# Denominator loads on SP's queue, and a ring model that shares by packet size, in a gated attention and GLU kernel

## Chip, cores and metric

The kernel runs on one core of one Trainium2 chip, as one program. The metric is the device time in microseconds, the median of several runs.

## What is computed

Two branches read the same input x (2048 tokens, 640 features) and are mixed by a gate per token. Branch a is linear attention with 32 heads of 20 columns; branch b is a GLU with a sigmoid gate, 1536 wide.

```python
def _A_ref(x, wqkv, wo):
    B, S, D = x.shape
    H = 32; Dh = D // H
    qkv = (x @ wqkv).reshape(B, S, 3, H, Dh).transpose(2, 0, 3, 1, 4)
    q, k, v = qkv[0], qkv[1], qkv[2]
    phi = lambda t: jnp.where(t > 0, t + 1, jnp.exp(t)) + 1e-6
    pq, pk = phi(q), phi(k)
    kv = jnp.einsum("bhsd,bhse->bhde", pk, v)
    z = jnp.einsum("bhsd->bhd", pk)
    num = jnp.einsum("bhqd,bhde->bhqe", pq, kv)
    den = jnp.einsum("bhqd,bhd->bhq", pq, z)[..., None] + 1e-6
    o = num / den
    return o.transpose(0, 2, 1, 3).reshape(B, S, D) @ wo

def _B_ref(x, w_gate, w_up, w_down):
    g = jnp.einsum("bsd,df->bsf", x, w_gate)
    u = jnp.einsum("bsd,df->bsf", x, w_up)
    h = _sigmoid(g) * u
    return jnp.einsum("bsf,fd->bsd", h, w_down)

g = _sigmoid((x * gate_w).sum(-1, keepdims=True))
return g * a + (1 - g) * b
```

## The kernel before

**Tiling and stages.** The 2048 tokens are four groups g of 512 (NG, TG), the 640 features five tiles of 128 (KC). Each large product is split into a high and a low part (`split`) and runs as three matmuls (`mm3`, lines 404 to 406); products of 2x2 blocks are made with seven products instead of eight, out of sums of tiles. In order of time:

- the first part: keys, phi(k) and the matrix `gt`; the sum of phi(k) gathers in `zacc`;
- `q_phase(1)` and `f_phase(1)`: queries and GLU for groups 2 and 3. The transformed weights are written to DRAM (`w_dram`, `wd_dram`);
- `q_phase(0)` and `f_phase(0)`: the same for groups 0 and 1. The weights come back from DRAM ready made, by `load_form` (tiles wg, wu, ws for step f) and `load_wf` (tile wf, the down weights of two steps);
- the attention output: phi(q), scaled by gate / denominator, times the matrix `m`.

An f_phase runs over f = 0 to 11, each a block of seven steps s1 to s7. For odd f above 1 the four pieces d0 to d3 of the down product of the previous two steps lie between them; they use wf. At f, steps 2, 6 and 7 the loads of wg, wu and ws for f + 2 are issued, and after step 7 of an odd f `load_wf`.

**The denominators.** `phi_q` writes phi(q) of tile u and group g to `p_dram`. `queue_dens(g, g')` (line 1399) puts the work for two groups in a row: `load` fetches a tile of phi(q) as `pden` (256 KB), `one` multiplies it by the column `zcol` and adds it to `fac[:, g]` on DVE and then asks for the tile after the next, five times; after the fifth the result goes to `den_dram`. `turn_in` reads it back with four small loads (64 KB each, pieces of 512 bytes) that put heads on other partitions, and loads `gs`, the gate. `factor` adds, inverts, multiplies by the gate and stores `fac_dram`; `turn_out` reads that back with four small loads on SP. It is called in `f_phase(0)` at f = 3 for groups 2 and 3 and at f = 7 for groups 0 and 1 (`dens`, line 2011). `queue_scale` uses the factors much later.

**What sets the order.** TensorE's order stands in the program text. The work of ACT and DVE waits in lists and is put between the matmuls by `Order`, while the program is written and not on the chip: it keeps a clock for each engine (`pe`, `act`, `vec`), and `fill` (line 115) takes the next piece if its operands are there by the plan (`ready`) and if it ends by the plan less than a slack after TensorE's clock (`_fits`). The denominators are in the list `chain`, the last but one; behind it in `spare` are the pieces of `queue_m`, which load `mr` tiles on SP. Within an engine the order on the chip is then fixed: an engine that waits for an operand holds up all that is written behind it.

**DMA queues in the plan.** There are two, SP's (`sp`) and POOL's (`gp`), each a `Ring` that issues its transfers in the order of the text. A transfer that must wait for a tile or for data holds up those behind it. `Ring.dma_start` works out when it is issued and how long it takes alone (`took`, from its bytes and the length r of its contiguous pieces); `Rings.issue` then runs both rings against each other and sets the time of landing that `order.when` returns. While both have a transfer under way, each has half of the engines.

```python
dt = min([left[k] * len(live) for k in live] + [c - t for c in coming])
...
took = 1.25 * max(1, n // r) * (7 + 0.0377 * r) / 16e3
```

Of the kernel before, what the change touches and what calls it, by code (L numbers as in the profile page):

```python
# [14 lines left out]
P = 128  # L15
# [287 lines left out]
class Rings:  # L303
# [1 line left out]
    def __init__(self):  # L305
        self.q = [[], []]

    def issue(self, n, arrive, took):
        cell = [0.0]
        self.q[n].append((arrive, took, cell))  # L310
        i, t, left = [0, 0], 0.0, [None, None]
        q = self.q
        while True:
            for k in range(2):
                if left[k] is None and i[k] < len(q[k]) and q[k][i[k]][0] <= t:
                    left[k] = q[k][i[k]][1]
            live = [k for k in range(2) if left[k] is not None]
            coming = [q[k][i[k]][0] for k in range(2) if left[k] is None and i[k] < len(q[k])]
            if not live:
                if not coming:  # L320
                    break
                t = min(coming)
                continue
            dt = min([left[k] * len(live) for k in live] + [c - t for c in coming])
            t += dt
            for k in live:
                left[k] -= dt / len(live)
                if left[k] <= 1e-9:
                    q[k][i[k]][2][0] = t + 0.5
                    left[k] = None  # L330
                    i[k] += 1
        return cell


class Ring:

    def __init__(self, engine, order, rings, n, issue, lag):
        self.engine, self.order, self.rings, self.n, self.issue, self.lag = engine, order, rings, n, issue, lag
        self.t = 0.0
# [12 lines left out]
    def dma_start(self, out, src, **kw):  # L352
        o = self.order
        start = max(self.t, o.data(out, [src]))
        self.t = start + self.issue
        (r1, n), (r2, _) = (self.run(ap, 0 if getattr(ap.tensor, "_space", DRAM) == DRAM else 1) for ap in (out, src))
        r = min(r1, r2)
        took = 1.25 * max(1, n // r) * (7 + 0.0377 * r) / 16e3
        self.cell = self.rings.issue(self.n, start + self.lag, took)
        o.put(out, [src], self.cell)  # L360
        return self.engine.dma_start(out, src, **kw)

# [5 lines left out]
def v_cost(w):  # L368
    return 0.07 + w / 960

@with_exitstack
def gated_mix_kernel(ctx: ExitStack, tc: tile.TileContext, xt, xn, wk, wv, wo, wst_q, wst_f, out_t):
# [8 lines left out]
    sp, gp = Ring(nc.sync, order, rings, 0, 0.38, 1.5), Ring(nc.gpsimd, order, rings, 1, 0.55, 2.2)  # L381
# [37 lines left out]
    def vec2(out, a, b, op, after=""):  # L419
        order.on_vec(width(out), after, 1.0, out, a, b)  # L420
        nc.vector.tensor_tensor(out, a, b, op=op)  # L421

    def vec3(out, a, scalar, b, op0, op1, after=""):
        order.on_vec(width(out), after, 1.0, out, a, b)
        nc.vector.scalar_tensor_tensor(out, a, scalar, b, op0=op0, op1=op1)

    def vec1(out, a, s0, s1=None, op0=OP.mult, op1=None, after=""):
        order.on_vec(width(out), after, 1.0, out, a)
        if op1 is None:
            nc.vector.tensor_scalar(out, a, s0, None, op0=op0)  # L430
        else:
            nc.vector.tensor_scalar(out, a, s0, s1, op0=op0, op1=op1)
# [10 lines left out]
    def add(out, a, b, after=""):  # L443
        vec2(out, a, b, OP.add, after)

    def sub(out, a, b, after=""):
        vec2(out, a, b, OP.subtract, after)
# [7 lines left out]
    fac = common.tile([P, NG, TG], F32, name="fac")  # L455
    p_dram = dram.tile([P, KC, NG, TG], F32, name="p_dram")
# [76 lines left out]
    class Chunk:  # L533
# [39 lines left out]
        def sum(self, n):  # L573
            x = self.x
            b11, b12, b21, b22 = x[0][:, 0:2], x[1][:, 0:2], x[0][:, 2:4], x[1][:, 2:4]
            self.T = (b11, b22, b12, b21)
            if n == 0:
                sub(b11, b12, b11)
            elif n == 1:
                sub(b12, b22, b12)  # L580
            elif n == 2:
                sub(b22, b22, b11)
            else:
                sub(b21, b21, b22)
# [434 lines left out]
    g = GTBatch(0, [0])  # L1019
# [8 lines left out]
    for c in range(1, 4):  # L1028
        ck = chunks[c]
        if c == 1:  # L1030
# [14 lines left out]
            g = GTBatch(c, batches[c])  # L1045
# [97 lines left out]
        if c > 1:  # L1143
            g = GTBatch(c, batches[c])
# [50 lines left out]
    def tt(name, dt=F32, shape=(P, TG)):  # L1195
        return pw.tile(list(shape), dt, name=name, tag="t", bufs=4)
# [202 lines left out]
    def queue_dens(*gs2):  # L1399

        st = {}

        def load(g, u):
            if u < KC:
                st[g, u] = tt("pden")
                gp.dma_start(st[g, u], p_dram[:, u, g])
                st["at", g, u] = lambda: order.when(st[g, u])

        def one(g, u):
            td = fac[:, g]  # L1410
            if u == 0:
                vec1(td, st[g, u], zcol[:, 0:1], zeps[:, 0:1], OP.mult, OP.add)
            else:
                vec3(td, st[g, u], zcol[:, u:u + 1], td, OP.mult, OP.add)
            load(g, u + 2)
            if u == KC - 1:
                gp.dma_start(den_dram[:, g], td)
                st["at", g, u + 1] = lambda: order.when(den_dram[:, g])

        def turn_in(g):  # L1420
            for j in range(4):
                js = slice(j * H, (j + 1) * H)
                gp.dma_start(fac[js, g].rearrange("h (d c) -> h d c", c=P),
                                  den_dram[:, g, j * P:(j + 1) * P].rearrange("(d h) c -> h d c", h=H))
            st[g, "gs"] = tt("gs")[:, :P]
            sp.dma_start(st[g, "gs"], gate_rep[4 * g:4 * g + 4].rearrange("i h c -> (i h) c"))
            st["at", g, KC + 1] = lambda: max(order.when(fac[:, g]), order.when(st[g, "gs"]))

        def factor(g):
            td = fac[:, g]  # L1430
            q = td[:, :P]
            add(td[:, :2 * P], td[:, :2 * P], td[:, 2 * P:])
            add(q, q, td[:, P:2 * P])
            order.on_vec(5 * P, "")
            nc.vector.reciprocal(q, q)
            vec2(q, q, st[g, "gs"], OP.mult)
            gp.dma_start(fac_dram[:, g], q)
            st["at", g, KC + 2] = lambda: order.when(fac_dram[:, g])

        def turn_out(g):  # L1440
            for d in range(4):
                sp.dma_start(fac[d * H:(d + 1) * H, g].rearrange("h (j c) -> h j c", c=P),
                                  fac_dram[:, g].rearrange("(j h) c -> h j c", h=H))
        order.add(0, 0, lambda: [load(g, u) for u in range(2) for g in gs2], chain=True)
        for u in range(KC):
            for g in gs2:
                order.add(0, v_cost(TG), lambda g=g, u=u: one(g, u), None, lambda g=g, u=u: st["at", g, u](), chain=True)
        for n, (v, fn) in enumerate(((0, turn_in), (2.0, factor), (0, turn_out))):
            for g in gs2:
                order.add(0, v, lambda g=g, fn=fn: fn(g), ("fac", g) if n == 2 else None,  # L1450
                          lambda g=g, n=n: st["at", g, KC + n](), chain=True)
# [751 lines left out]
    q = q_phase(1, lambda k: [(b12h[:, k], b12l[:, k])], extra)  # L2203
# [33 lines left out]
    q = q_phase(0, lambda k: [(c_h[c][:, k], c_l[c][:, k]) for c in range(2)], {})  # L2237
# [383 lines left out]
```

## Time and profile before

| what | us |
|---|---|
| median of 3 runs (lowest to highest) | 735.46 (735.04 to 735.61) |
| the profiled execution | 735.37 |
| its span | 733.6 |
| TensorE (PE) busy | 727.4 |
| VectorE (DVE) busy | 561.5 |
| ScalarE (ACT) busy | 358.6 |
| GpSimd (POOL) busy | 114.0 |

Times within the trace count from the start of the span. `f_phase(0)` with the denominators lies at about 420 to 625 us in it. In a row of the order of time, the first figure is the start, the second the duration, and what stands in square brackets is how long the engine was idle before it and what ended that. In a row of the waits, the figures are the total, the number of times and the longest. A row that begins with SPq or POOL and DMA_DIRECT2D is the issue of a transfer; the landing comes later. The rows of DMA issues end with the median time to landing. In a row of windows follow, after the stretch and its length, the busy times (with the number of instructions) of PE, the weight loads, DVE, ACT and POOL, then TensorE's granted clock, the busy share of the DMA engines and GB/s.

### The profile page before, as it was taken

The numbers are of one execution on the slowest core, as the hardware profiler recorded it, in microseconds if no ns is written. First come the engines' busy times: TensorE is split into PE (matmuls) and PEld (weight loads), VectorE is DVE, ScalarE is ACT, GpSimd is POOL, SyncE is SP. The second block draws the span as 40 slices with busy tenths as digits, with TensorE's granted clock in tenths as the row PEclk, the third lists the DMA queues.
The fourth block names the chain that finished last, engine by engine and source line by source line (L and its number), as shares of the span: only waits on it lengthen the run. The fifth ranks groups of instructions, "written<-read, shape, count | busy, mean of one in ns | idle before, by whom it ended". The sixth has DMA issues, their size and how long they took to land.

```text
span 733.6 us, 10128 instructions
## 1 busy us (share of the span) xinstructions
PE 727.4 (99%) x3575; PEld 623.3 (85%) x3575; DVE 561.5 (77%) x987; ACT 358.6 (49%) x668; POOL 114.0 (16%) x197
## 2 busy tenths in 40 slices
PE   9999999999999999999999999999999999999998
PEld 8999999988788888888888888888787888888886
DVE  4978787987677989898989973466766775688783
ACT  5765648358556653535355363454333232324550
POOL 0211111113211211111210033023011331000000
PEclk9999999999999999999999999999999999999999
DMA  8464648697877866457687289878968597759212
GB/s 270 119 189 120 186 108 250 151 334 284 295 271 264 327 240 242 183 215 257 256 326 265 102 291 373 321 240 280 363 242 326 172 324 204 273 207 347 76 69 101
DMA packets 68873, 173.54 MB, mean 237 GB/s; under 512 B 11690, under 2 KB 31418, under 8 KB 65238
## 3 DMA queue, kind: packets, MB, share of 16 engines
q1 hardware_dynamic: 50342, 103.70, 42.7%
q0 software_dynamic: 18336, 69.03, 26.7%
q8 instruction: 28, 0.46, 0.3%
q14 instruction: 23, 0.19, 0.1%
q10 hardware_dynamic: 144, 0.16, 0.1%
HBM read 103.96 MB, written 63.92 MB: 229 GB/s over the span
## 4 chain that ended last, share of the span: by engine, by line
PE 86%; DMA 6%; issue 4%; DVE 2%; ACT 1%; POOL 1%; SPq 0%; POOLq 0%; ACTq 0%; DVEq 0%
PE ch L404 9%; PE ch L406 9%; PE ch L405 9%; PE cc L404 7%; PE cc L405 7%; PE cc L406 7%; PE dd L404 7%; PE dd L406 7%; PE dd L405 7%; PE rot L404 6%; PE rot L406 5%; PE rot L405 5%; DMA mr<-m_dram 2%; DMA pden<-p_dram 2%; DMA wg<-wf 1%
## 5 line engine op out<-in xcount | busy, mean ns | idle before, releaser
L417 ACT ACTIVATE c<-ch 128x512 f32<-128x512 f32 x52 | 31.1, 598 | 91.4 <-PE ch L406 91.3
L421 DVE TENSOR_TENSOR hf<-c,hf 128x512 fp32r<-128x512 f32 x75 | 51.2, 688 | 21.1 <-ACT hf L417 20.7
L417 ACT ACTIVATE hf<-c 128x512 fp32r<-128x512 f32 x75 | 46.1, 624 | 26.0 <-DVE c L421 26.0
L421 DVE TENSOR_TENSOR c<-cc,c 128x512 f32<-128x512 f32 x40 | 27.6, 689 | 40.6 <-PE cc L406 29.2
L404 PE MATMUL ch<-xth,ws 128*128 128x512 f32 x112 | 43.8, 391 | 0.0
L406 PE MATMUL ch<-xth,ws 128*128 128x512 f32 x112 | 43.6, 389 | 0.0
L405 PE MATMUL ch<-xtl,ws 128*128 128x512 f32 x112 | 43.6, 389 | 0.0
L421 DVE TENSOR_TENSOR tb<-rot,tb 128x512 f32<-128x512 f32 (+1 forms) x61 | 39.5, 677 | 3.0 <-PE rot L406 3.0
L421 DVE TENSOR_TENSOR tb<-dd,tb 128x512 f32<-128x512 f32 x44 | 30.3, 688 | 9.4 <-PE dd L406 9.4
L404 PE MATMUL dd<-xrh,wg 128*128 128x512 f32 x90 | 35.2, 391 | 0.0
L406 PE MATMUL dd<-xrh,wg 128*128 128x512 f32 x90 | 35.1, 389 | 0.0
L405 PE MATMUL dd<-xrl,wg 128*128 128x512 f32 x90 | 35.0, 389 | 0.0
L417 ACT ACTIVATE c<-dd 128x512 f32<-128x512 f32 x22 | 13.1, 598 | 41.4 <-PE dd L406 41.4
L404 PE MATMUL cc<-xbh,ws 128*128 128x512 f32 x84 | 32.7, 389 | 0.0
L405 PE MATMUL cc<-xbl,ws 128*128 128x512 f32 x84 | 32.7, 389 | 0.0
L406 PE MATMUL cc<-xbh,ws 128*128 128x512 f32 x84 | 32.7, 389 | 0.0
L421 DVE TENSOR_TENSOR c<-c,c 128x512 f32<-128x512 f32 x46 | 31.6, 688 | 1.3 <-ACT c L417 0.7
L417 ACT ACTIVATE dd<-ch 128x512 f32<-128x512 f32 x22 | 12.8, 582 | 35.0 <-PE ch L406 35.0
L421 DVE TENSOR_TENSOR wst<-wst 128x256 f32<-128x256 f32 (+2 forms) x69 | 27.4, 413 | 1.5
L404 PE MATMUL rot<-pkh,xnh 128*128 128x320 f32 x90 | 28.1, 312 | 0.1
L405 PE MATMUL rot<-pkl,xnh 128*128 128x320 f32 x90 | 27.8, 309 | 0.0
L406 PE MATMUL rot<-pkh,xnl 128*128 128x320 f32 x90 | 27.8, 309 | 0.0
(650 smaller groups left out, 2350.8 us busy)
## 6 DMA issues: line engine op xcount, KB each, us to landing
wf<-ws POOLq DMA_DIRECT2D x12, 1152.0 KB, 7.7
ws<-wf SPq DMA_DIRECT2D x11, 1152.0 KB, 9.5
wst<-wst_f SPq DMA_DIRECT2D x12, 640.0 KB, 5.2
wf<-wg POOLq DMA_DIRECT2D x12, 640.0 KB, 6.4
wd<-wd POOLq DMA_DIRECT2D x12, 640.0 KB, 8.0
wg<-wf SPq DMA_DIRECT2D x12, 640.0 KB, 5.8
wf<-wd SPq DMA_DIRECT2D x10, 640.0 KB, 10.1
xnst<-xn SPq DMA_DIRECT2D x16, 320.0 KB, 4.3
```

What stands on the lines that cost most here:

```text
L404: nc.tensor.matmul(out, l_hi, r_hi, start=first, stop=False, skip_group_check=True)
L405: nc.tensor.matmul(out, l_hi, r_lo, start=False, stop=False, skip_group_check=True)
L406: nc.tensor.matmul(out, l_lo, r_hi, start=False, stop=last, skip_group_check=True)
L417: nc.scalar.activation(out, src, fn, **kw)
L421: nc.vector.tensor_tensor(out, a, b, op=op)
```

## The change

Three things change. The model of the rings shares the engines between two live transfers in proportion to a weight, 7 + 0.0377 r with r taken as at most 2600 bytes, in place of equal halves. The `pden` loads, twenty in all, are issued on SP's queue in place of POOL's. So are the sixteen loads of `turn_in`. The stores to `p_dram`, `den_dram` and `fac_dram` stay on POOL's queue.

```diff
-    def issue(self, n, arrive, took):
+    def issue(self, n, arrive, took, share):
         cell = [0.0]
-        self.q[n].append((arrive, took, cell))
+        self.q[n].append((arrive, took, cell, share))
...
-            dt = min([left[k] * len(live) for k in live] + [c - t for c in coming])
+            all_ = sum(q[k][i[k]][3] for k in live)
+            part = {k: q[k][i[k]][3] / all_ for k in live}
+            dt = min([left[k] / part[k] for k in live] + [c - t for c in coming])
             t += dt
             for k in live:
-                left[k] -= dt / len(live)
+                left[k] -= dt * part[k]
...
-        self.cell = self.rings.issue(self.n, start + self.lag, took)
+        self.cell = self.rings.issue(self.n, start + self.lag, took, 7 + 0.0377 * min(r, 2600))
...
         def load(g, u):
             if u < KC:
                 st[g, u] = tt("pden")
-                gp.dma_start(st[g, u], p_dram[:, u, g])
+                sp.dma_start(st[g, u], p_dram[:, u, g])
...
             for j in range(4):
                 js = slice(j * H, (j + 1) * H)
-                gp.dma_start(fac[js, g].rearrange("h (d c) -> h d c", c=P),
+                sp.dma_start(fac[js, g].rearrange("h (d c) -> h d c", c=P),
                                   den_dram[:, g, j * P:(j + 1) * P].rearrange("(d h) c -> h d c", h=H))
```

## Prediction

> **What bounds the kernel now.** The page first, for the engine that is full; then what that engine waited for; then the stretch around each wait on the engine that released it, and last the two DMA queues there.
>
> ```profile
> span 733.6 us, 10128 instructions
> PE 727.4 (99%) x3575; PEld 623.3 (85%) x3575; DVE 561.5 (77%) x987; ACT 358.6 (49%) x668; POOL 114.0 (16%) x197
> PE rot L404 <- DVE tb L421: 0.9, 1, 0.9
> PE rot L492 <- PEq L2612: 0.8, 1, 0.8
> PE ch L404 <- ACT cx L417: 0.4, 1, 0.4
> PE dd L404 <- DMA wf<-wd: 0.2, 1, 0.2
> PE dd L404 <- ACT ms L417: 0.2, 1, 0.2
> ```
>
> TensorE is the bound: 727.4 of 733.6 us. The change adds and removes no matmul, so it can only fill or open gaps between matmuls. The waits are few: 0.8 us is the start, and 1.7 us lie inside, in four places. These figures are too small, because a matmul lasts 0.39 us in this trace while the next one starts 0.23 us after it, so 0.16 us of every gap is covered by the matmul still running. I therefore read gaps from start to start, in the order of time on TensorE:
>
> ```profile
> 518.87 0.39 PE L406 MATMUL ch<-xth,ws 128*128 128x512 f32 x1
> 519.49 0.50 PE L404 MATMUL dd<-hf,wf 128*128 128x512 f32 x1 [0.23 <-DMA wf<-wd]
> ...
> 567.58 0.40 PE L405 MATMUL cc<-hf,wf 128*128 128x512 f32 x1
> 567.82 0.39 PE L406 MATMUL cc<-hf,wf 128*128 128x512 f32 x1
> 569.14 0.47 PE L404 MATMUL rot<-hf,wf 128*128 128x512 f32 x1 [0.94 <-DVE tb L421]
> ```
>
> From 567.58 to 567.82 is the normal pitch, 0.24. From 567.82 to 569.14 is 1.32, so 1.08 is lost; from 518.87 to 519.49 is 0.62, so 0.38 is lost. Both lie in the stretches in which the denominators are made (f of 3 and of 7 in the second f_phase). Why DVE was late at 568 is in its order of time:
>
> ```profile
> 555.88 0.99 DVE L432 TENSOR_SCALAR fac<-pden,zcol,zeps 128x512 f32<-128x512 f32 x2
> ...
> 563.38 0.75 DVE L425 SCALAR_TENSOR_TENSOR fac<-pden,zcol,fac 128x512 f32<-128x512 f32 x1 [2.38 <-DMA pden<-p_dram]
> ...
> 567.05 0.74 DVE L425 SCALAR_TENSOR_TENSOR fac<-pden,zcol,fac 128x512 f32<-128x512 f32 x1
> 567.71 0.69 DVE L421 TENSOR_TENSOR c<-cc,c 128x512 f32<-128x512 f32 x1
> 568.31 1.28 DVE L421 TENSOR_TENSOR tb<-rot,tb 128x512 f32<-128x512 f32 x2
> ```
>
> DVE works strictly in its written order. A denominator step was written ahead of its operand's landing, DVE stood still for 2.38 us, ran without a pause from there, and gave the rot bank back 1.08 us late. That is the one stall that the moved operations visibly cause.
>
> **The change, part by part.** *The ring model* issues nothing. It changes predicted landings only where both rings carry data at once with unlike pieces: 512 bytes against 2600 and more now get 26.3/(26.3+105), 20%, where they had 50%; 2048 bytes get 44%. TensorE's order is fixed in the text, so what can change is the order on ACT and DVE, anywhere in the kernel. Bounds: it may remove the gaps outside these stretches (0.4 and 0.2 in the list above, with the covered 0.16 each some 0.9 us together), and it may open a gap as large as the largest there is now, 1.1 us, or two of them. I take 0.
>
> *Twenty pden loads* leave POOL's queue for SP's, and *sixteen turning loads* (four per group) with them.
>
> ```profile
> L361 POOL DMA_DIRECT2D pden<-p_dram x20: 537/537/549, 449.2 to 568.1; - x20
> L361 POOL DMA_DIRECT2D fac<-den_dram x16: 549/549/572, 500.6 to 583.8; - x16
> L361 SPq DMA_DIRECT2D fac<-fac_dram x16: 302/348/424, 525.3 to 606.8; - x16
> 449.18 1.61 POOL L361 DMA_DIRECT2D pden<-p_dram  x3
> 539.22 2.15 POOL L361 DMA_DIRECT2D pden<-p_dram  x4
> 555.27 0.32 SPq L361 DMA_DIRECT2D ws<-wf  x1
> ```
>
> POOL saves 36 issues of about 0.54, 19.5 us, and gains nothing on the path by it: it is busy 16%. SP pays 36 issues of 0.35, 12.6 us (the turning out, whose shape is that of the turning in, is the nearest row). They are hidden as long as SP stands waiting for tiles that TensorE frees, which from 555.6 on it does for 21 us.
>
> What matters is the place in the queue. POOL ran ahead: the first loads went out at 449.2 and 539.2, long before their first use (481.8 and 555.9). SP reaches the same lines only behind ws at 481.20 and 555.27. For the pair 0, 1: ws (1152 KB) and four loads (1024 KB) at the best rate in the windows below (390 GB/s) take 3.0 and 2.7 us, with some 2 us to land, so operands come from 561 to 563 at the earliest; by the medians of the page (9.5 for ws, 6.2 for pden) at 565 to 571. The chain starts 5 to 10 us later than today. Nothing near waits for it: the factors are first used on DVE from 636.5 on. The loads now queue behind known transfers of their own ring, and the 1 MB leaves the stretch 540 to 560, where the DMA engines are full, for 560 to 580, where they are not:
>
> ```profile
> 500.00:520.00 20.00, 19.77 (x87) 16.06 (x87) 13.95 (x24) 7.41 (x14) 6.56 (x12) 1.00 0.97 325
> 540.00:560.00 20.00, 20.00 (x90) 16.55 (x89) 11.25 (x19) 8.26 (x16) 2.97 (x6) 1.00 1.02 390
> 560.00:580.00 20.00, 19.06 (x85) 15.43 (x84) 16.53 (x27) 3.75 (x7) 4.79 (x9) 1.00 0.44 152
> ws<-wf SPq DMA_DIRECT2D x11, 1152.0 KB, 9.5
> pden<-p_dram POOLq DMA_DIRECT2D x20, 256.0 KB, 6.2
> L425 DVE SCALAR_TENSOR_TENSOR pl<-pl,fac x9: 683/689/690, 636.5 to 665.7; 128x512 f32<-128x512 f32 x9
> ```
>
> So I take the stall at 568 away whole: -1.08 us. Its bounds are -1.08 and 0 (DVE waits as long in another place).
>
> *Pair 2, 3* is the tight one. Here is what SP does there, and what it waits for from 509 to 522:
>
> ```profile
> 481.20 0.32 SPq L361 DMA_DIRECT2D ws<-wf  x1
> ...
> 501.71 1.39 SPq L361 DMA_DIRECT2D gs<-gate_rep  x2
> 503.15 0.42 SPq L361 DMA_DIRECT2D wu<-wf  x1
> 503.65 0.40 SPq L361 DMA_DIRECT2D wg<-wf  x1
> 505.69 0.32 SPq L361 DMA_DIRECT2D ws<-wf  x1
> 506.05 1.83 SPq L361 DMA_DIRECT2D wf<-wd  x3
> 507.98 4.38 SPq L361 DMA_DIRECT2D mr<-m_dram  x4
> 515.96 0.34 SPq L361 DMA_DIRECT2D wu<-wf  x1
> 500.65 4.37 POOL L361 DMA_DIRECT2D fac<-den_dram  x8
> SPq L361 <- DMA ws<-wf: 3.5, 1, 3.5
> 525.32 7.72 SPq L361 DMA_DIRECT2D fac<-fac_dram  x8
> ```
>
> The wu load at 515.96 waited 3.5 us for ws to land, with which it shares no tile; ws is eight issues before it (ws, three wf, four mr). I read this as at most eight transfers under way on the queue, so every small load takes a place. Turning in goes out today at 500.65; 5 to 10 us later is 505.7 to 510.7, and the wf load that TensorE waits for at 519.49 goes out at 506.05. Behind wf the turning costs nothing, and the DMA engines (0.97 busy there) are relieved of it while wf lands: up to -0.38. Ahead of it, eight issues of 0.35 are 2.8 us, and with their wait for den_dram as much as the turning out took with its own, 7.72. If the engines have enough bytes of wu and wg meanwhile, part of that is covered. Bounds -0.38 and +7.7; I take half of the gain, -0.2, since the delay that I work out puts most of the interval behind 506.05.
>
> The Trainium skill, page DMA: Bandwidth & Descriptors, section "Issuing engines are not separate DMA queues", says that transfers issued from sync and GpSimd end on the same 16 engines and that another issuer saves only issue time. By that the change would be worth the POOL issue time alone, off the path: nothing. The rows agree as to bytes; the rival of a mere shift below is what it would give.
>
> **The sum.** The profiled execution took 735.37 us for a span of 733.6, so 1.77 lie around it; it stands 0.09 under the median 735.46. 735.37 - 1.08 - 0.2 + 0 = 734.1; with the 0.09 it is 734.2.
>
> **Rivals.** *(1) Slower: turning in gets ahead of ws and wf at 505.7.* It is written as soon as the plan thinks den_dram landed; if that is before the end of f = 3, step 7, SP waits for the real landing, issues ten loads, and wf starts 2.8 to 7.7 us late. It starts to cost at once, as TensorE waits for wf already today. Net of the 1.08: +1.7 to +6.6, middle +4: 739.4; with part of it covered by other bytes, 737 to 738. For it: the interval touches 505.7. Against it: the same bytes already compete today, from POOL, and cost 0.38.
> *(2) A mere shift:* the chain is written ahead of the landing again, DVE waits elsewhere, or the same bytes land no sooner from another queue, and the time stays at 735.4. For it: the model knows no limit of eight. Against it: from 560 to 580 the engines are 0.44 busy.
> *(3) The new order on ACT and DVE opens gaps elsewhere,* two of 1.1 us beside the gain lost: 737.5. For it: DVE is 77% busy and every landing is recomputed. Against it: apart from three short gaps the old model's plan held everywhere.
> *(4) All inner gaps close:* 1.08 + 0.38 + 0.9 = 2.4 us, 733.1.
>
> **How the numbers follow.** Forecast 40%, (1) 23%, (2) 15%, (3) 10%, (4) 12%. A difference under 0.2%, 1.47 us, can't be told from no change here, so faster means under 734.0 and slower over 736.9. The forecast's own range is 733.7 to 735.2; three tenths of it lie under 734.0: 12%. Faster 12 + 12 = 24%; same 28 + 14 + 1 = 43%; slower 23 + 9 + 1 = 33%. The range for 8 in 10 runs from (4), 733.0, into the upper part of (1), 739.5.
>
> **What would show it.** Right: no DVE wait on pden over 1 us and no gap near 568; first pden of the second pair after 555.6 on SP; wf at or before 506.1 and no wait for it at 519. Wrong: turning in between wg at 503.65 and wf, and a TensorE wait on wf or ws of f = 5 over 1 us; or new TensorE waits on DVE or ACT before 440, where nothing is moved.

## The result and the profile after

The changed kernel takes 733.14 us (median of 8 runs, 732.57 to 734.73) against 735.54 for the kernel before beside it (8 runs): ratio 0.9977, interval 0.9967 to 0.9986. Two more comparisons of the same program gave 0.9985 (0.9973 to 0.9998) and 0.9985 (0.9976 to 0.9994). Ratios here and below are the recorded ones and not quotients of two medians, which differ a little (0.9967 for the first). By the ratios the change is faster by 1.1 to 1.7 us, which is a little under or over the 0.2% that the prediction took for the least that can be told; by the medians it is 2.4, 1.1 and 0.6 us.

The profiled execution took 733.22 us for a span of 731.3, against 735.37 and 733.6. These are what TensorE waited for after the change, in total, times, and longest (the changed kernel's text is two lines longer, so its L406 is L404 of before):

```profile
PE rot L494 <- PEq L2614: 0.8, 1, 0.8
PE rot L406 <- DVE tb L423: 0.4, 1, 0.4
PE dd L406 <- ACT ms L419: 0.2, 1, 0.2
```

Of the four inner waits of before, three are gone: DVE at 568, wf at 519 and ACT at 196. One is new. Measured from start to start, and counting every gap over 0.13 us after the first 10 us, the gaps of before add up to 2.86 us and those of after to 1.44. The new one is here, in TensorE's order of time and then in DVE's:

```profile
495.76 0.39 PE L408 MATMUL dd<-hf,wf 128*128 128x512 f32 x1
496.54 0.50 PE L406 MATMUL rot<-hf,wf 128*128 128x512 f32 x1 [0.39 <-DVE tb L423]
```

```profile
487.75 1.22 DVE L434 TENSOR_SCALAR fac<-pden,zcol,zeps 128x512 f32<-128x512 f32 x2 [0.76 <-DMA pden<-p_dram]
489.18 0.75 DVE L427 SCALAR_TENSOR_TENSOR fac<-pden,zcol,fac 128x512 f32<-128x512 f32 x1 [0.21 <-DMA pden<-p_dram]
490.71 0.75 DVE L427 SCALAR_TENSOR_TENSOR fac<-pden,zcol,fac 128x512 f32<-128x512 f32 x1 [0.78 <-DMA pden<-p_dram]
...
495.13 0.75 DVE L427 SCALAR_TENSOR_TENSOR fac<-pden,zcol,fac 128x512 f32<-128x512 f32 x1 [0.34 <-DMA pden<-p_dram]
495.80 1.28 DVE L423 TENSOR_TENSOR tb<-rot,tb 128x512 f32<-128x512 f32 x2
...
567.27 0.54 DVE L434 TENSOR_SCALAR fac<-pden,zcol,zeps 128x512 f32<-128x512 f32 x1
```

The mechanism of 568 now costs time with the other pair of groups: DVE waits four times for pden, the sum that frees the rot bank comes at 495.80, and TensorE loses 0.55. A wait on pden is not new there. DVE before:

```profile
489.69 1.42 DVE L425 SCALAR_TENSOR_TENSOR fac<-pden,zcol,fac 128x512 f32<-128x512 f32 x2 [1.35 <-DMA pden<-p_dram]
491.70 0.75 DVE L425 SCALAR_TENSOR_TENSOR fac<-pden,zcol,fac 128x512 f32<-128x512 f32 x1 [0.60 <-DMA pden<-p_dram]
...
495.69 1.28 DVE L421 TENSOR_TENSOR tb<-rot,tb 128x512 f32<-128x512 f32 x2
```

It waited about as long and TensorE lost nothing, since four of the ten steps were done before 486 and six stood between there and that sum. After the change the chain starts at 487.75, and eight steps stand ahead of the sum. For the second pair there is no wait on pden at all, and its chain starts at 567.27. On SP's queue:

```profile
479.86 0.32 SPq L363 DMA_DIRECT2D ws<-wf  x1
480.27 1.84 SPq L363 DMA_DIRECT2D mr<-m_dram  x4
482.23 9.59 SPq L363 DMA_DIRECT2D pden<-p_dram  x8
...
505.38 2.23 SPq L363 DMA_DIRECT2D wf<-wd  x3
509.63 1.72 SPq L363 DMA_DIRECT2D mr<-m_dram  x4
513.51 8.89 SPq L363 DMA_DIRECT2D fac<-den_dram  x4
...
557.97 17.41 SPq L363 DMA_DIRECT2D pden<-p_dram  x9
```

The turning in comes at 513.5, behind wf, and TensorE no longer waits for wf.

Another part of the difference in span lies in the first 8 us. There the order of every engine is unchanged, yet the profiles of all the kernels below stand 0.2 to 1.0 us ahead of the profile of before at that point (0.55 for the changed kernel, and 0.3 in each of two more profiles of the same program). Two profiles of one program, the change with a margin of 2.0, differ by 0.8 us there, so I take it for scatter of single executions, with the profile of before at the slow end.

### The profile page after: what moved, and what is told of

It is laid out like the page before. It is cut to its first block, busy times and chain, and to the rows that moved or that the text cites. A ratio compares the mean times of both kernels' runs of the same rounds, so it can differ in the third digit from the quotient of the medians.

```text
span 731.3 us, 10111 instructions
## 1 busy us (share of the span) xinstructions
PE 726.0 (99%) x3575; PEld 622.6 (85%) x3575; DVE 561.3 (77%) x987; ACT 358.4 (49%) x668; POOL 94.7 (13%) x161
## 4 chain that ended last, share of the span: by engine, by line
PE 85%; DVE 5%; DMA 4%; issue 2%; ACT 2%; POOL 1%; SPq 0%; DVEq 0%; POOLq 0%; ACTq 0%
PE ch L406 9%; PE ch L407 9%; PE ch L408 9%; PE cc L406 8%; PE cc L408 8%; PE cc L407 8%; PE dd L406 6%; PE dd L407 6%; PE dd L408 6%; PE rot L406 5%; PE rot L408 5%; PE rot L407 5%; DMA wo_sb<-wo 1%; DMA pden<-p_dram 1%; DVE gt L423 1%
## 5 line engine op out<-in xcount | busy, mean ns | idle before, releaser
L406 PE MATMUL ch<-xth,ws 128*128 128x512 f32 x112 | 43.7, 390 | 0.0
L406 PE MATMUL dd<-xrh,wg 128*128 128x512 f32 x90 | 35.2, 391 | 0.0
L406 PE MATMUL cc<-xbh,ws 128*128 128x512 f32 x84 | 32.7, 389 | 0.0
L406 PE MATMUL rot<-pkh,xnh 128*128 128x320 f32 x90 | 28.1, 312 | 0.1
```

The source lines that it names most:

```text
L406: nc.tensor.matmul(out, l_hi, r_hi, start=first, stop=False, skip_group_check=True)
```

## The experiments

All are timed against the kernel before on the same chip. "Margin" is time added to the landing of pden that the plan believes; it moves no transfer to another queue and changes the order on DVE alone at first hand.

| kernel | median us | before beside it | ratio, 95% interval | gaps over 0.13 in one profile, us |
|---|---|---|---|---|
| ring model alone | 737.84 | 735.43 | 1.0030 (1.0020 to 1.0040) | 4.94 |
| pden on SP alone | 735.48 | 735.43 | 1.0004 (0.9991 to 1.0018) | 4.7, and 1.5 of slower matmuls |
| turning in on SP alone | 737.96 | 735.43 | 1.0034 (1.0023 to 1.0045) | 4.44 |
| both moves, old model | 734.75 | 735.43 | 0.9993 (0.9984 to 1.0002) | 2.48 |
| the change again | 734.15 | 735.22 | 0.9985 (0.9973 to 0.9998) | 2.39 |
| the change, margin 2.0 | 733.31 | 735.22 | 0.9972 (0.9962 to 0.9982) | 0.72 |
| the change, margin 1.0 | 733.71 | 735.22 | 0.9981 (0.9971 to 0.9991) | 1.02 |
| kernel before, margin 2.5 | 733.55 | 735.22 | 0.9978 (0.9969 to 0.9986) | 2.14 |
| the change a third time | 734.27 | 734.89 | 0.9985 (0.9976 to 0.9994) | 2.59 |
| the change, margin 2.0, again | 733.00 | 734.89 | 0.9970 (0.9959 to 0.9981) | 0.73 |
| ring model alone, margin 2.5 | 735.58 | 734.89 | 1.0004 (0.9994 to 1.0015) | 3.15 |
| both moves, old model, margin 2.0 | 733.45 | 734.89 | 0.9980 (0.9970 to 0.9989) | 3.54 |

**Ring model alone.** The lines of `Rings` and `Ring` from the diff, nothing else.

> The ring model alone; pden and the turning in stay on POOL. Theory A (each part closes its own gaps): the gap at 196 us (0.56 from start to start, and its after-effects, 0.7 in all) goes, the gaps at 519 and 568 stay: about 734.8, ratio 0.999. Rival B (the model's gain is the whole gain, the queue does not matter): 733.1 to 733.5, gap at 568 gone too. Rival C (a new order without the moves opens other gaps: here the factor of group 2 is written ahead of the sum of f = 4, and waits for the turning in): 1 to 4 us slower than before, a DVE wait on fac or gs near 505 to 510 us.

It is 0.3% slower: rival C. The gap at 196 is closed. In the old plan ACT had the split of ws ahead of a copy out of TensorE's bank, and waited 2.18 us for DVE there; in the new one the copy comes first. ACT before, and then with the model alone:

```profile
195.55 0.74 ACT L417 ACTIVATE ws<-wst 128x640 fp32r<-128x640 f32 x1 [2.18 <-DVE wst L421]
196.20 0.58 ACT L417 ACTIVATE cx<-ch 128x512 f32<-128x512 f32 x1
```

```profile
194.41 0.60 ACT L417 ACTIVATE cx<-ch 128x512 f32<-128x512 f32 x1 [1.66 <-PE ch L406]
```

But without the moves the same model writes the next split of mr and the factor of group 2 ahead of the sum of f = 4 (`c<-cc,c`) on DVE, where that sum stood first. DVE before, and then with the model alone:

```profile
505.69 0.69 DVE L421 TENSOR_TENSOR c<-cc,c 128x512 f32<-128x512 f32 x1 [2.79 <-PE cc L406]
506.35 0.82 DVE L421 TENSOR_TENSOR mt<-mr,mt 128x640 fp32r<-128x640 f32 x1
```

```profile
507.30 0.82 DVE L421 TENSOR_TENSOR mt<-mr,mt 128x640 fp32r<-128x640 f32 x1 [5.71 <-ACT mt L417]
508.04 0.74 DVE L421 TENSOR_TENSOR fac<-fac 128x256 f32<-128x256 f32 x2
...
510.01 0.68 DVE L421 TENSOR_TENSOR c<-cc,c 128x512 f32<-128x512 f32 x1
```

ACT's part of that split waited for its load:

```profile
506.53 0.74 ACT L417 ACTIVATE mt<-mr 128x640 fp32r<-128x640 f32 x1 [5.66 <-DMA mr<-m_dram]
507.17 0.58 ACT L417 ACTIVATE c<-dd 128x512 f32<-128x512 f32 x1
```

ACT stood 5.66 us before a load that the plan thought had landed, and the copies behind it came late; TensorE lost 0.78 at 507. ACT's order there is that of the kernel before, where the same split waited 3.92 us and TensorE lost nothing, so this gap comes of a later landing of mr; why it landed later is open. The 0.76 at 511 comes of DVE's new order: the sum at 510.01 and ACT's piece behind it were late. The gaps at 530 stand behind a split of mr again, which ACT began at 528.36 after a wait of 3.88. The waits are on mr, not on fac or gs as I had written. The stall at 568 is still there (0.88).

**The moves apart.** One word each: `gp` to `sp` in `load`, in `turn_in`, or in both.

```diff
-                gp.dma_start(st[g, u], p_dram[:, u, g])
+                sp.dma_start(st[g, u], p_dram[:, u, g])
```

> The pden loads alone on SP, old model, turning in on POOL. Theory A: the gap at 568 (1.09) and the one at 519 (0.39) go, one of 0.5 at 496 comes, the gap at 196 stays: about 734.5, ratio 0.9987. Rival (the stall at 568 comes from the bytes, not from the place in the order): DVE waits for pden over 1 us again, 735.4.

> The turning in alone on SP, old model, pden on POOL. Here the eight small loads of groups 2 and 3 are written ahead of wu, ws and wf of f = 5, which is the first rival of the prediction. Theory: SP issues wf 2.8 to 7.7 us later than 506.05 and TensorE waits for it at 519: 1.5 to 7 us slower than before, 737 to 742. Against it: the bytes of wu and wg cover the delay, 735.4, with the gap at 568 unchanged.

> Both moves, old model. The order on DVE and ACT is that of the pden move alone; only the queue of the turning in differs. Theory A: as the pden move alone or up to 0.4 faster, 734.1 to 734.5; the gap at 196 is there. Rival (the model is needed for the moves to pay): 735.4 or slower.

*pden alone* is no faster. The gaps at 568 and 519 go as expected, but what comes at 496 is not 0.5. In the profiled execution, the slowest of its twelve (738.59), DVE waited 3.11 and 1.21 us for the first two pden:

```profile
491.09 0.55 DVE L432 TENSOR_SCALAR fac<-pden,zcol,zeps 128x512 f32<-128x512 f32 x1 [3.11 <-DMA pden<-p_dram]
492.84 0.55 DVE L432 TENSOR_SCALAR fac<-pden,zcol,zeps 128x512 f32<-128x512 f32 x1 [1.21 <-DMA pden<-p_dram]
```

*The turning in alone* is the prediction's first rival made real, and 0.34% slower. Its queue, and what TensorE waited for:

```profile
500.44 2.53 SPq L361 DMA_DIRECT2D fac<-den_dram  x4
...
506.89 2.84 SPq L361 DMA_DIRECT2D mr<-m_dram  x4
509.82 0.38 SPq L361 DMA_DIRECT2D ws<-wf  x1
510.24 3.65 SPq L361 DMA_DIRECT2D wf<-wd  x3
```

```profile
PE ch L404 <- DMA ws<-wf: 1.6, 1, 1.6
PE rot L404 <- DVE tb L421: 1.0, 1, 1.0
```

wf goes out at 510.24 instead of 506.05, 4.2 us late and inside the 2.8 to 7.7 that I had worked out. The turning alone is 2.8 of it (wu goes out at 505.94 instead of 503.15); the rest comes with four mr loads, at 507.98 and behind wf before, which now stand ahead of ws. ws is as late, and it is ws that TensorE misses first, with a gap of 1.79. A late issue isn't always paid: with the ring model alone wf went out at 510.97 and TensorE did not wait for it. The stall at 568 is unchanged (1.16).

*Both moves without the model* can't be told from before (0.9993, interval up to 1.0002). The turning falls behind wf, since the chain is late enough; the gaps at 519 and 568 go, one of 1.16 comes at 496, and the gap at 196 stays.

**Is it the queue or the order?** A margin on the landing, in the changed kernel (2.0 and 1.0 us) and in the kernel before (2.5):

```diff
-                st["at", g, u] = lambda: order.when(st[g, u])
+                st["at", g, u] = lambda: order.when(st[g, u]) + 2.0
```

> The changed kernel once more (the same program, with its two added lines folded into others), beside the next ones. Expected 733.1 as first measured, ratio 0.9967 to 0.9986; in its profile the gap at 196 gone, a wait on pden and a gap of 0.5 to 1.5 at 496, no gap at 519 and 568.

> The changed kernel with 2.0 us added to the landing that the plan believes for pden. Theory (DVE is late at 496 because the step is written ahead of its operand's landing, by 0.8 to 3.1 us): no DVE wait on pden over 0.5 us, the gap at 496 goes, 0.5 to 1.2 us faster than the changed kernel: 731.9 to 732.6. Rival (DVE is simply full there): the gap stays, 733.1, or another opens because the chain ends later.

> The same with 1.0 us. Theory: between the two, the wait on pden shorter than 1.5 us, 732.2 to 733.0. Rival: 733.1.

> The kernel before with 2.5 us added to the plan's landing of pden, and nothing else: the loads and the turning in stay on POOL, the old ring model. Theory (the stall at 568 is a step written too early, and any plan that knows the real landing removes it): gap at 568 gone, those at 196 and 519 unchanged, 1.1 us faster than before, 734.3, ratio 0.9985. Rival (only the other queue removes it, since POOL's loads compete with the weights): gap at 568 stays, 735.4.

The kernel before with the margin alone, both kinds of loads still on POOL, reaches 0.9978, as much as the whole change. In its profile the stall at 568 is gone, by order alone:

```profile
563.43 0.69 DVE L421 TENSOR_TENSOR tb<-ch,tb 128x512 f32<-128x512 f32 x1
564.11 0.69 DVE L421 TENSOR_TENSOR tb<-cc,tb 128x512 f32<-128x512 f32 x1
564.72 0.74 DVE L425 SCALAR_TENSOR_TENSOR fac<-pden,zcol,fac 128x512 f32<-128x512 f32 x1
```

Three sums for TensorE's banks now stand ahead of the denominator step that had held DVE at 563.38, and the step finds its operand there. 0.9978 is 1.6 us, more than the 1.1 of that gap, and 733.55 is 0.75 below the time that I had written. That profile even has a new gap of 0.66 at 508, behind a wait of 5.57 us for mr on ACT as with the model alone, and what makes up the rest is open.

The change again had 1.71 us of gap at 496, behind DVE waits on pden of 1.60 and 1.40. With the margin of 2.0 that gap is gone and no other came; this is all that TensorE then waits for:

```profile
PE rot L492 <- PEq L2612: 0.8, 1, 0.8
PE dd L404 <- ACT ms L417: 0.2, 1, 0.2
PE rot L404 <- DVE gt L421: 0.2, 1, 0.2
```

With 1.0 the longest DVE wait on pden is 0.3 us and the gap at 496 is gone too. Both times, 733.31 and 733.71, lie above what I had written (731.9 to 732.6 and 732.2 to 733.0), as the change itself took 1.0 us more than in its first comparison; against it beside them they are 0.8 and 0.4 less, and the 0.4 is within the scatter. The change with the margin of 2.0 is only 0.24 below the kernel before with its margin, which can't be told apart.

**Which parts are needed beside a margin.** The same line, put into the ring model alone and into the two moves with the old model, and the pair from above once more.

> The changed kernel a third time, for a direct comparison on one chip with the next three: 733.1 to 734.2; its wait on pden before 496 varies from run to run, and with it the gap there (0.5 to 1.7).

> The changed kernel with 2.0 us added to the planned landing of pden, again. Theory: no gap at 496 in any profile, 0.5 to 1.5 us faster than the changed kernel beside it. Rival: the difference of the first comparison was chance, and the two are equal.

> The new ring model with 2.5 us added to the planned landing of pden, everything on POOL's queue as before. If the queue is not needed: gaps at 196 and 568 gone, 732.8 to 733.6, as good as the changed kernel. If the model needs the move to SP (alone it wrote the splits of mr ahead of their landing at 500 to 510): gaps of 0.7 at 507 and 511 as in the model alone, 735 to 737.

> Both moves on SP with 2.0 us added to the planned landing of pden, old ring model. Theory: as the changed kernel with the margin, less the gap at 196 that only the new model closes: 0.7 us slower than that one, 733.5 to 734.2, no gap at 496. Rival: without the model the moves open other gaps, 735.

On one chip the change takes 734.27 and the change with the margin 733.00, after 734.15 and 733.31 in the comparison before: 1.3 and 0.8 us less, both times with no gap at 496 in the profile. Its interval (0.9959 to 0.9981) and that of the change (0.9976 to 0.9994) still overlap at the edge, and so they do in the comparison before; the two comparisons and the profiles point the same way. It has the lowest ratios of this study (0.9972 and 0.9970).

The model with the margin but without the moves is no faster than before. The gaps at 507 and 511 of the model alone don't come back; instead SP's queue holds four mr loads ahead of ws and the gate load gs ahead of wf:

```profile
504.72 1.79 SPq L361 DMA_DIRECT2D mr<-m_dram  x4
506.56 1.10 SPq L361 DMA_DIRECT2D ws<-wf  x1
507.82 0.37 SPq L361 DMA_DIRECT2D gs<-gate_rep  x1
508.24 1.83 SPq L361 DMA_DIRECT2D wf<-wd  x3
```

```profile
PE dd L404 <- DMA wf<-wd: 2.2, 2, 1.3
```

wf is 2.2 us later than the 506.05 of before, and TensorE loses 1.42 and 1.05. So neither answer that I had written fits: the queue is not what closes 568, but in this profile, without the moves, the new plan's order on SP comes with late weights for f = 5. That the late issue alone makes them late is not shown (510.97 cost nothing with the model alone).

The moves with the margin and the old model take 733.45, at the lower edge of the 733.5 to 734.2 expected. Their profile, of an execution of 736.16 that is far above their median, has no gap at 496 and keeps the one at 196 (0.52), but TensorE waited there 0.9 us for ws and 1.0 for wf at 517 and 522. How often that happens, one profile doesn't show.

## Why the prediction was right, and where not

*The direction and the range* held: 734.2 was forecast, 733.14 measured beside its first comparison and 734.15 and 734.27 in the others, all inside 733.0 to 739.5. The forecast's own range, 733.7 to 735.2, holds the later two and misses the first by 0.6. That the sum came so near is in part luck: 2.0 us of gaps closed (1.08, 0.38 and 0.56) where 1.28 was forecast, and 0.6 to 1.7 opened at 496 where nothing was. The first median is the number of the fourth rival, 733.1, but not its case, as not all the gaps closed. Of the signs of being right, the places on SP's queue hold in the first profile, and its longest DVE wait on pden is 0.78; in the other two it is 1.60 and 2.29, over the 1 us that was named.

*The stall at 568, taken away whole (-1.08).* The mechanism was right, and the margin on the kernel before shows it with nothing else altered: a step was written ahead of its operand's landing. The reason given for why the moves would cure it was wrong. "The loads now queue behind known transfers of their own ring" is what failed: the plan did not know that landing either. The first pden went out at 482.23 and DVE could use it at 487.75. In three profiles of the same program the first pden of groups 2 and 3 kept DVE waiting 0.76, 1.60 and 2.29 us, and TensorE lost 0.55, 1.71 and 1.61 at 496. There the second rival, to which I gave 15%, came true for one pair of groups. For the other pair the start at 567.27, 11.4 us later than before where I had said 5 to 10, put the steps behind the landing. The moves without the model show no gain that can be measured, and the gap of 1.16 at 496 in their profile fits that.

*wf at 519 (half of 0.38).* The whole came: no gap at 519, with wf issued at 505.38 and the turning in at 513.51, 12.9 us later than before instead of 5 to 10. The first rival's condition was put rightly, by the place of the turning against ws and wf, and its price too (4.2 us on the queue, 2.8 of them the turning's own); TensorE paid 1.79 of them in that profile, and first for ws, which I had not counted.

*The ring model, taken at 0.* That term was mis-sized. It closed the gap at 196, 0.56 from start to start, which is in the fourth rival and its -0.9; its bound on the other side, "as large as the largest there is now, 1.1 us, or two of them", was reached, but only without the moves: five gaps of 0.39 to 0.81 and 0.3% slower alone. The three parts don't add. Alone they give +0.3%, 0 and +0.34%; together they give -0.15 to -0.23%. Each alters the order that the others are put into; that this is the whole reason is argued, not shown.

*The Trainium skill's rule* (DMA: Bandwidth & Descriptors, "Issuing engines are not separate DMA queues") says that another issuer saves issue time only. The kernel before with the margin agrees with it: 0.9978 with nothing moved, 0.9977 and 0.9985 with 36 loads moved. No run here measures how fast the two queues move the same bytes, and the place in a queue does count: the turning alone put wf 4.2 us back and was 0.34% slower.

## What to carry to other kernels

Where a kernel's order is written out from a plan, a wait of one in-order engine on a transfer means that the plan puts the landing earlier than it comes. Such a wait need not cost the full engine anything (the two on pden at 489 to 492 before cost nothing), so look for those behind which it stands. Correct the planned landing, or add a margin where nothing near needs the result, before moving transfers between queues; here 2.5 us added on one line of the kernel before did as much as the whole change, and 2 us on that line of the changed kernel another 0.8 to 1.3 us on top of it. Small loads on a queue that also feeds the full engine can be paid by whatever is written behind them, so look first at the next load that this engine waits for.

## What the runs showed of the hardware

When the pden move alone had its longest stall, TensorE stood for 3.33 us and then ran slower. A window ahead of that stall and one behind it, with TensorE's granted clock as the last figure but two:

```profile
490.00:496.00 6.00, 6.00 (x28) 4.99 (x27) 3.50 (x6) 3.79 (x7) 0.00 (x0) 1.00 0.56 167
500.00:504.00 4.00, 3.54 (x10) 2.79 (x11) 2.93 (x5) 2.10 (x4) 0.21 (x1) 0.63 0.48 159
```

```profile
500.46 0.50 PE L404 MATMUL rot<-hf,wf 128*128 128x512 f32 x1 [3.33 <-DVE tb L421]
...
501.43 0.63 PE L404 MATMUL rot<-hf,wf 128*128 128x512 f32 x1
501.85 0.63 PE L405 MATMUL rot<-hf,wf 128*128 128x512 f32 x1
...
504.67 0.39 PE L406 MATMUL ch<-xth,wu 128*128 128x512 f32 x1
504.89 0.39 PE L404 MATMUL ch<-xth,wu 128*128 128x512 f32 x1
```

The granted clock was 0.63 in the mean over those 4 us, and matmuls started 0.42 us apart instead of 0.23 until 504.4; eight of them cost another 1.5 us. Behind the gap of 1.71 us at 496 in the changed kernel's second profile the window 500 to 504 has a clock of 1.00. The Trainium skill, page TensorE: Matmul & The Clock Gate, section "What's actually happening", states that an idle window of about 3.4 us throttles TensorE to half its clock and that about as long a busy one releases it; the trace agrees, with 3.33 us of waiting, a pitch of 0.42 in place of 0.23, and some 4 us to recover.

What the prediction read as a limit of eight transfers under way shows again in the changed kernel: three pden went out from 482.23 on, and the fourth, eight issues behind ws, only at 485.96 in the first profile, after SP had waited 2.3 us for ws to land. The kernel's plan has no such limit. It can bear on the fourth pden, for which DVE waited 0.78 at 490.71, but not on the first, which is waited for as well. Whether the limit is one of the chip or of the program that issues, no run shows, and that the landings would be on time without it wasn't tried.
